# Expert remainders in pieces of 64 and twice 32 rows, four column groups, and the weights of two layers loaded apart

## The chip, the cores and the metric

The kernel runs on one core of one Trainium2 chip. A core has TensorE (PE in the profile, with its weight loads shown apart as PEld), VectorE (DVE), ScalarE (ACT), GpSimd (POOL) and SyncE (SP), which here issues most of the transfers. All data are 32-bit floats. The metric is the device time of one execution in microseconds (us). Most executions agree within 0.3%.

## The reference

The computation has two blocks, one behind the other. The first is causal attention over 8 batches, 8 heads, 576 positions and 64 elements a head, with a bias that grows with the running sum of a gate:

```python
scores = scale * np.matmul(q, k.transpose(0, 1, 3, 2))
cum = np.cumsum(np.maximum(s, 0.0), axis=-1)
bias = -(cum[:, :, :, None] - cum[:, :, None, :])
scores = np.where(causal, -1000000000.0, scores + np.minimum(bias, 0.0))
attn = softmax(scores)           # exp(scores - max) / (sum + 1e-9)
attn_out = np.matmul(attn, v)    # becomes x: 8 x 576 tokens of 512
```

The second is a layer of 8 experts. Each of the 4608 tokens goes to exactly one expert, either the one with the highest logit or, where a local gate says so, the one that the token before it went to:

```python
e = fresh_e if s == 0 or local_gate[b, s] < 0.5 else prev_e
h = np.maximum(x[b, s] @ w1[e], 0.0)     # w1[e]: 512 x 1024
out[b, s] = p[e] * (h @ w2[e])           # w2[e]: 1024 x 512
```

How many tokens an expert gets depends on the data. The inputs come from a fixed seed, so it is the same in each run.

## The kernel before

**Attention** (`attention`, L670 to L1035) takes 32 pairs of heads. Scores are computed transposed (L873), exponentiated on ScalarE (L874), masked on GpSimd (L859) and multiplied with the weighted values (L900). The exponentials are taken without subtracting a maximum, so this fast form holds only within a range of the gate sums. While it runs, the router (`Router`, L109 to L404) finds the expert of each token and scatters the token's row into a table in memory that has one region per expert (L308).

**Counting and assigning.** All shapes in the program are fixed, but the number of rows of an expert is not. So the program holds a fixed list of units, `ORDER` (L52), and the router works out on the chip, from the counts, which expert and which rows each unit gets. There are three kinds of unit. D takes 256 rows of one expert, S 128 rows of one expert, and M takes two pieces of 64 rows, which may belong to two experts. 14 D, 4 S and 6 M make 38 slots of 128 rows; 4608 rows are 36. `assign` (L339) hands out the places of one size: from `n`, the pieces that each expert wants, and `k`, the places there are, it computes the expert and first row of each place, how many pieces each expert got, and the running sum `end` of what was wanted. D's are handed out first, partly ahead of time (`EARLY`), then S's, then halves. The pieces wanted come from the counts by a shift (`shifted`, L327), for halves after adding 63, so that the last piece is rounded up:

```python
n = self.shifted("n3", 6, HALF - 1)                       # L400
v.scalar_tensor_tensor(n, self.used, -2.0, n, Alu.mult, Alu.add)
self.parts, _, end = self.assign("d", n, self.start, UNITS_OF["H"], HALF)
v.tensor_scalar(self.over, end[:, E - 1 :], -float(UNITS_OF["H"]), 0.0, Alu.add, Alu.max)   # L404
```

**The units' work** (`Experts`, L407 to L667). For a unit, SP fetches its rows from the table (`fetch`, L470, L481), VectorE turns them in blocks of 32 (`turn_x`, L501), and SP loads the weights of the expert: `load` (L454, L467), 2 MB for layer 1 and 2 MB for layer 2. For D and S, layer 1 keeps the weights in TensorE and moves the rows (L525). For M, the rows are kept instead, 64 columns wide in one of two column groups, and the weights of the two experts move through them (L516). Its result is turned back by VectorE (`turn_h`, L536). Layer 2 (L551) keeps the rows and moves the weights, for M again in two column groups. VectorE multiplies with the gate (L554) and GpSimd scatters the rows to the output (L556); rows that fill up a unit without belonging to a token are not written.

**The order** is written out by hand (`run`, L564). An M is interleaved with the unit ahead of it: layer 1 of both, then layer 2 of both. There are four places for weights; a load goes to a place (`place`, L451) when the unit that used it is through. `loads` issues the next loads, both layers of one at once, as soon as that unit is in `done`; the fourth place opens only when the last rows have been scattered to the table. SP runs its queue in order.

**The guard.** `in_range` (L1048) checks that the fast attention was in range, adds `over`, the halves that were wanted beyond the 12 there are, and writes `out_of` (L1067). At the end every engine loads it and branches (L92 to L94):

```python
with tc.If(wrong > 0):
    attention_general(tc, q, k, vm, vt, s, w_gate, w_local, cum_d, x_d, ident, lg)   # L104
    route(tc, ident, lg, ebi, idx_g, idx_s, gate)
    experts_general(tc, w1, w2, out, x_d, ident, ebi, idx_g, idx_s, gate)            # L106
```

The general kernel computes the whole output for any input: attention with a row maximum (L1071 to L1303; for each pair of heads, scores in five steps, sums and maxima on VectorE, exponentials on ScalarE, transposes through TensorE, then the values; the inputs q, k and v of a batch have one buffer), routing (L1307), and 43 blocks of 128 rows (L1472 to L1548), each of two layers of eight 512-column products and twelve transposes.

Of the kernel before, what the change touches and what calls it, by code (L numbers as in the profile page):

```python
# [17 lines left out]
P = 128  # L18
B, H, S, DH = 8, 8, 576, 64
D = H * DH  # L20
# [27 lines left out]
EMPTY = 1 << 20  # L48
DOUBLE, SINGLE, HALF = 2 * P, P, P // 2
EARLY = (2, 3)  # L50
UNITS_OF = {"D": 14, "S": 4, "H": 12}
ORDER = "DDDDD" + "MDD" * 3 + "MDS" * 2 + "MDSS"  # L52
PLACES = 4
# [55 lines left out]
class Router:  # L109
# [273 lines left out]
    def assign_doubles(self):  # L383
        v = self.nc.vector
        self.counted()
        n = self.shifted("n1", 8)
        v.tensor_tensor(n, n, self.used, op=Alu.subtract)
        v.tensor_scalar(self.start, self.used, float(DOUBLE), None, Alu.mult)
        self.doubles, used, _ = self.assign("b", n, self.start, UNITS_OF["D"] - sum(EARLY), DOUBLE)
        v.tensor_tensor(self.used, self.used, used, op=Alu.add)  # L390
        v.tensor_scalar(self.start, self.used, float(DOUBLE), None, Alu.mult)

    def assign_rest(self):
        v = self.nc.vector
        n = self.shifted("n2", 7)
        v.scalar_tensor_tensor(n, self.used, -2.0, n, Alu.mult, Alu.add)
        self.singles, used, _ = self.assign("c", n, self.start, UNITS_OF["S"], SINGLE)
        v.scalar_tensor_tensor(self.used, self.used, 2.0, used, Alu.mult, Alu.add)
        v.tensor_scalar(self.start, self.used, float(SINGLE), None, Alu.mult)
        n = self.shifted("n3", 6, HALF - 1)  # L400
        v.scalar_tensor_tensor(n, self.used, -2.0, n, Alu.mult, Alu.add)
        self.parts, _, end = self.assign("d", n, self.start, UNITS_OF["H"], HALF)
        self.over = self.t("over", [P, 1])
        v.tensor_scalar(self.over, end[:, E - 1 :], -float(UNITS_OF["H"]), 0.0, Alu.add, Alu.max)  # L404


class Experts:  # L407
    def __init__(self, ctx, tc, w1, w2, out, table, router):
        self.ctx, self.tc, self.nc = ctx, tc, tc.nc
        self.w1, self.w2, self.out, self.table, self.router = w1, w2, out, table, router  # L410

        def pool(name, bufs):
            return ctx.enter_context(tc.tile_pool(name=name, bufs=bufs))

        self.w_first = pool("w_first", 1)
        self.xqs = pool("xqs", 2)
        self.xts = pool("xts", 2)
        self.sm = pool("sm", 4)
        self.x_stack = ExitStack()
        self.p_x = self.x_stack.enter_context(tc.tile_pool(name="p_x", bufs=2 * GB, side="right"))  # L420
        self.puts = []
        self.units = []
        count = {"D": 0, "S": 0, "M": 0}
        loads = 0
        for kind in ORDER:
            n = 2 if kind == "M" else 1
            self.units.append((kind, count[kind], list(range(loads, loads + n))))
            count[kind] += 1
            loads += n
        assert count == {"D": UNITS_OF["D"], "S": UNITS_OF["S"], "M": UNITS_OF["H"] // 2}  # L430
        self.owner = {l: u for u, (_, _, ls) in enumerate(self.units) for l in ls}
        self.ws, self.xq, self.gi, self.xT, self.hT, self.hs = {}, {}, {}, {}, {}, {}

    def piece(self, u, i, row):
        kind, n, _ = self.units[u]
        if kind == "D":
            if n < sum(EARLY):
                i = int(n >= EARLY[0])
                of, n = self.router.early[i], n - i * EARLY[0]
            else:  # L440
                of, n = self.router.doubles, n - sum(EARLY)
        elif kind == "S":
            of = self.router.singles
        else:
            of, n = self.router.parts, 2 * n + i
        return self.nc.values_load(of[0:1, row, n : n + 1], engines=[ET.SP], min_val=0,
                                   max_val=E * CAP if row else E - 1,
                                   skip_runtime_bounds_check_because="clamped when it was counted")
# [4 lines left out]

    def load(self, l, part=None):  # L454

        if l not in self.owner:
            return
        nc, u = self.nc, self.owner[l]
        if not part:
            pool = getattr(self, self.place(l))  # L460
            self.ws[l] = pool.tile([P, DK, F], F32, name="w1b"), pool.tile([P, FK, D], F32, name="w2b")
            self.e = self.piece(u, self.units[u][2].index(l), 0)
        parts = 1 if part is None else 4
        for t, src in zip(self.ws[l], (self.w1, self.w2)):
            n = t.shape[1] // parts
            c = slice((part or 0) * n, (part or 0) * n + n)
            nc.sync.dma_start(t[:, c].rearrange("p c f -> p (c f)"),  # L467
                              src[bass.ds(self.e, 1), :, c].rearrange("o p c f -> (o p) (c f)"))

    def fetch(self, u):  # L470
# [6 lines left out]
        gi = self.gi[u] = self.sm.tile([P, 2, 2], F32, name="gi")  # L477
        pieces = 2 if kind == "M" else 1

        def get(to, of):  # L480
            self.tc.add_to_no_dep_group("gets", nc.sync.dma_start(to, of).ins)  # L481

        size = {"D": DOUBLE, "S": SINGLE, "M": HALF}[kind]
        for i in range(pieces):
            r = self.piece(u, i, 1)
            src = self.table[bass.ds(r, size)]
            t = size // 32
            for a in range(4):
                get(xq[32 * a : 32 * a + 32, i * t : i * t + t, :],
                                  src[:, a, :].rearrange("(t i) f -> i t f", i=32))  # L490
            p = min(size, P)
            get(gi[i * HALF : i * HALF + p, :n, :],
                              src[:, 0, XW - 2 :].rearrange("(n p) f -> p n f", p=p))

    def turn_x(self, u):
        if u >= len(self.units):
# [5 lines left out]
                                 xq[:, :n, : P].rearrange("p t (c i) -> p t c i", i=32))  # L502

    def layer1(self, u, c):
        nc, mm = self.nc, self.nc.tensor.matmul
        kind, _, ls = self.units[u]
        xT = self.xT[u]
        if kind == "M":
            if c == 0:
                self.hs[u] = self.fp.tile([P, F], F32, name="hs")  # L510
            if c < 2:
                ps = self.ps_m.tile([P, 512], F32, name="hp", tag="m")
                for k in range(DK):
                    for i in range(2):
                        d = slice(HALF * i, HALF * i + HALF)
                        mm(ps[d, :], lhsT=xT[:, k, d], rhs=self.ws[ls[i]][0][:, k, c * 512 : c * 512 + 512],  # L516
                           start=(k == 0), stop=(k == DK - 1))
                nc.scalar.activation(self.hs[u][:, c * 512 : c * 512 + 512], ps, Act.Relu)  # L518
# [10 lines left out]
    def turn_h(self, u):  # L529
        if self.units[u][0] != "M":  # L530
            return
# [8 lines left out]
    def layer2(self, u, between=None):  # L540
# [4 lines left out]
        for n in range(2 if kind == "D" else 1):  # L545
            ps = self.ps_y.tile([P, D], F32, name="yp")
            for k in range(FK):
                for i in range(2 if kind == "M" else 1):
                    w = HALF if kind == "M" else P
                    d = slice(i * w, i * w + w)  # L550
                    mm(ps[d, :], lhsT=hT[:, k, n * P + i * w : n * P + i * w + w], rhs=self.ws[ls[i]][1][:, k, :],  # L551
                       start=(k == 0), stop=(k == FK - 1))
# [11 lines left out]
    def run(self, recs, wend, out_of):  # L564
# [44 lines left out]
        self.load(2)  # L609
        loaded, done, fetched, freed = 3, set(), 2, False  # L610

        def loads():
            nonlocal loaded, freed
            while loaded in self.owner:
                if before.get(loaded) is not None and self.owner[before[loaded]] not in done:
                    return
                if self.place(loaded) == "w_last" and not freed:
                    if self.puts or todo:
                        return
                    self.x_stack.close()  # L620
                    self.w_last = pool("w_last", 1, side="right")
                    freed = True
                self.load(loaded)
                loaded += 1

# [14 lines left out]
        while u < len(kinds):  # L640
            if u + 1 < len(kinds) and kinds[u + 1] == "M":
                order += [(1, u), (1, u + 1), (2, u), (2, u + 1)]
# [4 lines left out]
        for what, u in order:  # L647
            if what == 1:
# [9 lines left out]
                if u:  # L658
                    self.turn_x(u + 1)
                    if u + 3 < first or not (self.puts or todo):  # L660
                        fetches(u + 3)
                        loads()
            else:
                self.layer2(u, lambda: between(u))
                done.add(u)
                loads()
        assert not todo and not self.puts  # L667


def attention(ctx, tc, q, k, vm, vt, vT, s, wbd_in, ident, recs, wend, router, experts):  # L670
# [290 lines left out]
    for i in range(4):  # L961
        plan(n + 9 + i, 3, lambda i=i: experts.load(0, i))
    plan(n + 12, 1, lambda: (experts.fetch(0), experts.fetch(1)))
# [643 lines left out]
```

## Time and profile before

| what | us |
|---|---|
| median of 3 runs | 774.21 (773.25 to 776.68) |
| the profiled execution | 774.9 |
| its span, first to last instruction | 773.1 |
| TensorE busy in the span | 760.7 |
| attention, up to the first expert product | 234.5 |
| expert products, 234 to 766: TensorE busy | 532.0 |
| end after the last product | 7 |

In the profile, a line such as `L551 PE MATMUL` names the line of the kernel. A 32-bit product is shown as two records, so `x16` in the chain of work is eight products. The chain is the work that ended last, followed back from the end; a slice line shows the busy share of 40 equal slices in tenths; a DMA line shows a queue's packets, its MB, and its share of the 16 DMA engines' time.

### The profile page before, as it was taken

Reading aid. Unit: us, or ns where it says so; the run is one execution under the profiler, and the core shown is the slowest. Engines: PE = TensorE matmul, PEld = TensorE weight load, DVE = VectorE, ACT = ScalarE, POOL = GpSimd, SP = SyncE. Lnnn points to the kernel's source line nnn. Section 1 sums busy time; section 2 is a strip of 40 time slices with the busy share of each in tenths; the row PEclk is TensorE's granted clock in tenths of the full one; section 3 lists DMA queues with packets and bytes.
Section 4 is the critical chain, followed back from the end, with each engine's and each line's share of the span. In section 5 each row is a group of like instructions: output and inputs, shape, how many; then the busy total and the mean of one; then the engine's idle time right before and its main releaser. Section 6 shows DMA issues by size and latency. Waiting matters only on the chain.

```text
span 773.1 us, 15685 instructions
## 1 busy us (share of the span) xinstructions
PE 760.7 (98%) x6319; PEld 512.9 (66%) x6319; DVE 247.4 (32%) x690; ACT 163.2 (21%) x315; POOL 216.1 (28%) x457
## 2 busy tenths in 40 slices
PE   8999999999999999999999999999999999999996
PEld 5887888888787657656376456737554664664664
DVE  5645655656644532110401320040113005005010
ACT  4454345344341001001010100101010110110111
POOL 3662276586666245430101010000101011001000
PEclk9999999999999999999999999999999999999999
DMA  8756557758678877639389739937982995996900
GB/s 299 270 204 219 184 165 257 231 172 301 203 245 325 277 272 268 235 87 413 96 341 391 235 115 430 382 99 272 420 276 54 412 382 174 418 383 220 404 16 32
DMA packets 57298, 196.74 MB, mean 254 GB/s; under 512 B 11901, under 2 KB 33149, under 8 KB 48000
## 3 DMA queue, kind: packets, MB, share of 16 engines
q1 hardware_dynamic: 50336, 175.55, 63.2%
q0 software_dynamic: 6880, 20.10, 6.7%
q8 instruction: 52, 0.85, 0.5%
q14 instruction: 30, 0.25, 0.1%
HBM read 175.00 MB, written 21.14 MB: 254 GB/s over the span
## 4 chain that ended last, share of the span: by engine, by line
PE 95%; DVE 2%; POOL 1%; issue 1%; ACT 1%; POOLq 0%
PE yp L551 34%; PE hp L525 29%; PE po L900 13%; PE ps L873 11%; PE hp L516 5%; PE vwp L814 1%; POOL e L859 1%; PE warm L747 0%; ACT e L874 0%; POOL table L308 0%; DVE vg L832 0%; DVE xb L908 0%; PE pos L260 0%; DVE mi L226 0%; PE lp L192 0%
## 5 line engine op out<-in xcount | busy, mean ns | idle before, releaser
L551 PE MATMUL yp<-w2b,hT 128*128 128x512 f32 (+1 forms) x704 | 267.4, 594 | 0.0
L525 PE MATMUL hp<-xT,w1b 128*128 128x256 f32 (+1 forms) x1152 | 226.0, 357 | 0.0
L525 PEld LDWEIGHTS hp<-xT,w1b 128*128 128x128 f32 x1152 | 198.8, 190 | 32.5 <-issue 9.9
L551 PEld LDWEIGHTS yp<-w2b,hT 128*128 128x128 f32 (+1 forms) x704 | 110.2, 175 | 148.8 <-issue 146.8
L556 POOL DMA_INDIRECT out_dram<-y,gi x38 | 37.1, 975 | 431.8 <-DVE y L554 367.5
L527 ACT ACTIVATE hT<-hp 128x256 f32<-128x256 f32 (+1 forms) x144 | 51.8, 359 | 435.7 <-PE hp L525 306.3
L554 DVE TENSOR_SCALAR y<-yp,gi 128x512 f32<-128x512 f32 x38 | 28.3, 744 | 296.1 <-PE yp L551 296.1
L874 ACT ACTIVATE e<-ps 128x768 f32<-128x768 f32 (+1 forms) x128 | 97.5, 837 | 109.5 <-PE ps L873 102.5
L900 PE MATMUL po<-vg,e 128*64 128x75 f32 x3200 | 116.0, 229 | 1.6 <-issue 1.4
L900 PEld LDWEIGHTS po<-vg,e 128*64 128x64 f32 x3200 | 108.8, 136 | 6.4 <-issue 2.8
L873 PE MATMUL ps<-qb,kb 64*128 64x192 f32 (+4 forms) x768 | 98.6, 400 | 1.6 <-DVE recs L906 1.2
L873 PEld LDWEIGHTS ps<-qb,kb 64*128 64x128 f32 x768 | 67.7, 187 | 32.9 <-ACT e L874 9.7
L308 POOL DMA_INDIRECT table<-xb,idx x72 | 74.0, 1028 | 28.8 <-issue 26.3
L859 POOL TENSOR_SCALAR_AFFINE_SELECT e<-e 128x256 f32<-128x256 f32 (+1 forms) x160 | 63.7, 425 | 51.6 <-ACT e L874 50.5
L536 DVE STREAM_TRANSPOSE hT<-hs 32x256 f32<-32x256 f32 x96 | 41.8, 436 | 108.6 <-ACT hs L518 107.3
L516 PE MATMUL hp<-w1b,xT 128*64 128x512 f32 x192 | 42.5, 595 | 0.0
L906 DVE RECIPROCAL recs<-po 128x12 f32<-128x12 f32 x64 | 13.2, 207 | 80.7 <-PE po L900 75.6
L908 DVE TENSOR_TENSOR xb<-po,recs 128x384 f32<-128x384 f32 x64 | 29.3, 458 | 3.9 <-POOL gap L307 1.1
L516 PEld LDWEIGHTS hp<-w1b,xT 128*64 128x64 f32 x192 | 13.3, 137 | 25.5 <-issue 25.3
L832 DVE TENSOR_TENSOR vg<-va,wk 128x1024 f32<-128x1024 f32 (+1 forms) x21 | 29.7, 1416 | 0.7 <-DMA va<-in_vm_dram 0.7
L501 DVE STREAM_TRANSPOSE xT<-xq 128x1024 f32<-128x1024 f32 (+1 forms) x24 | 24.4, 1016 | 0.6 <-issue 0.4
L307 POOL COPY gap<-recs 1x1 f32<-1x1 f32 x39 | 11.1, 284 | 30.9 <-DVE recs L906 30.9
(218 smaller groups left out, 185.9 us busy)
## 6 DMA issues: line engine op xcount, KB each, us to landing
w1b<-in_w_dram SPq DMA_DIRECT2D x29, 2048.0 KB
w2b<-in_w_dram SPq DMA_DIRECT2D x29, 2048.0 KB
kb<-in_k_dram SPq DMA_DIRECT2D x32, 288.0 KB
qb<-in_q_dram SPq DMA_DIRECT2D x32, 288.0 KB
vTb<-in_vT_dram SPq DMA_DIRECT2D x7, 1280.0 KB
xq<-table SPq DMA_DIRECT2D x56, 130.0 KB
va<-in_vm_dram SPq DMA_DIRECT2D x7, 1024.0 KB
w1b<-in_w_dram SPq DMA_DIRECT2D x4, 512.0 KB
```

Source lines behind the costliest of these rows:

```text
L308: put = self.nc.gpsimd.indirect_dma_start(out=self.halves, in_=src, element_offset=0, in_offset=None, out_offset=bass.IndirectOffsetOnAxis ...
L516: mm(ps[d, :], lhsT=xT[:, k, d], rhs=self.ws[ls[i]][0][:, k, c * 512 : c * 512 + 512], start=(k == 0), stop=(k == DK - 1))
L525: mm(ps[:, :w], lhsT=self.ws[ls[0]][0][:, k, c * P : c * P + P], rhs=xT[:, k, :w], start=(k == 0), stop=(k == DK - 1))
L527: nc.scalar.activation(self.hT[u][:, c, :w], ps[:, :w], Act.Relu)
L536: self.nc.vector.transpose(hT[32 * a : 32 * a + 32, :, 32 * r : 32 * r + 32], hs[32 * r : 32 * r + 32].rearrange("p (c i) -> p c i", i=P)[ ...
L551: mm(ps[d, :], lhsT=hT[:, k, n * P + i * w : n * P + i * w + w], rhs=self.ws[ls[i]][1][:, k, :], start=(k == 0), stop=(k == FK - 1))
L556: put = nc.gpsimd.indirect_dma_start(out=self.out[:, :], out_offset=bass.IndirectOffsetOnAxis(ap=gi.bitcast(I32)[:, n, 0:1], axis=0), in_= ...
L832: nc.vector.tensor_tensor(vgs[b % 2][g][:, c0:c1].rearrange("p c h e -> p (c h) e")[:, :, :DH], va[:, c0:c1].rearrange("p c h e -> p (c h) ...
L859: nc.gpsimd.affine_select(out=ap, in_=ap, compare_op=Alu.is_ge, fill=0.0, base=base, pattern=n, channel_multiplier=-1)
L873: mm(ps[:, h, at : at + z - a], lhsT=kb[d, key : key + P], rhs=qb[d, a:z], start=True, stop=True)
L874: nc.scalar.activation(e, ps, Act.Exp, scale=scale)
L900: mm(po[d, j - j0, :], lhsT=weights_of(n, c, j, h), rhs=vg[:, c, 2 * hp + h, :], start=(c == 0), stop=(c == last))
```

## The change

The remainder of an expert, what is left after its pieces of 256 and 128 rows, goes into pieces of 64 and of 32 rows. A new unit, T, holds one piece of 64 and two of 32 rows. In a T the rows stand in four column groups of 32, where the first two belong to the piece of 64 (`groups`). The list of units becomes a string of 25, written out. It holds 16 D, 5 S, 1 M and 3 T, which is 41 slots of 128 rows by count; the summary that came with the change speaks of 37 slots in place of 38. `UNITS_OF` is now counted from the string. `assign_rest` hands out halves after rounding the count down, then quarters after rounding up, and `over` is what is wanted of quarters beyond the places. `load` can load one layer's weights alone, and `loads` keeps two positions, one per layer: the first layer's weights of a load may be asked for once layer 1 of the unit that held the place is through.

```diff
-DOUBLE, SINGLE, HALF = 2 * P, P, P // 2
+DOUBLE, SINGLE, HALF, QUARTER = 2 * P, P, P // 2, P // 4
-UNITS_OF = {"D": 14, "S": 4, "H": 12}
-ORDER = "DDDDD" + "MDD" * 3 + "MDS" * 2 + "MDSS"
+PIECES = {"D": (DOUBLE,), "S": (SINGLE,), "M": (HALF, HALF), "T": (HALF, QUARTER, QUARTER)}
+ORDER = "DDDDDTDDDTDDDTDDMDSDSDSSS"
+UNITS_OF = {size: sum(PIECES[u].count(size) for u in ORDER) for size in (DOUBLE, SINGLE, HALF, QUARTER)}
...
-        self.singles, used, _ = self.assign("c", n, self.start, UNITS_OF["S"], SINGLE)
+        self.singles, used, _ = self.assign("c", n, self.start, UNITS_OF[SINGLE], SINGLE)
         v.scalar_tensor_tensor(self.used, self.used, 2.0, used, Alu.mult, Alu.add)
         v.tensor_scalar(self.start, self.used, float(SINGLE), None, Alu.mult)
-        n = self.shifted("n3", 6, HALF - 1)
+        n = self.shifted("n3", 6)
         v.scalar_tensor_tensor(n, self.used, -2.0, n, Alu.mult, Alu.add)
-        self.parts, _, end = self.assign("d", n, self.start, UNITS_OF["H"], HALF)
+        self.parts, used, _ = self.assign("d", n, self.start, UNITS_OF[HALF], HALF)
+        v.scalar_tensor_tensor(self.used, self.used, 2.0, used, Alu.mult, Alu.add)
+        v.tensor_scalar(self.start, self.used, float(HALF), None, Alu.mult)
+        n = self.shifted("n4", 5, QUARTER - 1)
+        v.scalar_tensor_tensor(n, self.used, -2.0, n, Alu.mult, Alu.add)
+        self.quarters, _, end = self.assign("q", n, self.start, UNITS_OF[QUARTER], QUARTER)
         self.over = self.t("over", [P, 1])
-        v.tensor_scalar(self.over, end[:, E - 1 :], -float(UNITS_OF["H"]), 0.0, Alu.add, Alu.max)
+        v.tensor_scalar(self.over, end[:, E - 1 :], -float(UNITS_OF[QUARTER]), 0.0, Alu.add, Alu.max)
...
-    def load(self, l, part=None):
+    def load(self, l, layer=None, part=None):
...
+        for i, src in enumerate((self.w1, self.w2)):
+            if layer is not None and layer != i:
+                continue
...
+    def groups(self, u):
+
+        kind, _, ls = self.units[u]
+        w = {"M": HALF, "T": QUARTER}.get(kind, P)
+        at = [l for l, size in zip(ls, PIECES[kind]) for _ in range(min(size, P) // w)]
+        return [(slice(i * w, i * w + w), l) for i, l in enumerate(at)]
...
                 for k in range(DK):
-                    for i in range(2):
-                        d = slice(HALF * i, HALF * i + HALF)
-                        mm(ps[d, :], lhsT=xT[:, k, d], rhs=self.ws[ls[i]][0][:, k, c * 512 : c * 512 + 512],
+                    for d, l in self.groups(u):
+                        mm(ps[d, :], lhsT=xT[:, k, d], rhs=self.ws[l][0][:, k, c * 512 : c * 512 + 512],
                            start=(k == 0), stop=(k == DK - 1))
...
         def loads():
-            nonlocal loaded, freed
-            while loaded in self.owner:
-                if before.get(loaded) is not None and self.owner[before[loaded]] not in done:
-                    return
...
+            more = True
+            while more:
+                more = False
+                for layer in range(2):
+                    l = loaded[layer]
+                    if l in self.owner and (not layer or l < loaded[0]) and ready(l, layer):
+                        self.load(l, layer)
+                        loaded[layer] += 1
+                        more = True
...
-            if u + 1 < len(kinds) and kinds[u + 1] == "M":
+            if u + 1 < len(kinds) and kinds[u + 1] in "MT":
...
             else:
                 self.layer2(u, lambda: between(u))
-                done.add(u)
-                loads()
+            done[what - 1].add(u)
+            loads()
```

More of the change, by code (lines that the diff above doesn't have):

```diff
@@ L388, in assign_doubles @@
         v.tensor_scalar(self.start, self.used, float(DOUBLE), None, Alu.mult)
-        self.doubles, used, _ = self.assign("b", n, self.start, UNITS_OF["D"] - sum(EARLY), DOUBLE)
+        self.doubles, used, _ = self.assign("b", n, self.start, UNITS_OF[DOUBLE] - sum(EARLY), DOUBLE)
         v.tensor_tensor(self.used, self.used, used, op=Alu.add)
@@ L422, in __init__ @@
         self.units = []
-        count = {"D": 0, "S": 0, "M": 0}
+        count = dict.fromkeys(UNITS_OF, 0)
         loads = 0
         for kind in ORDER:
[L426 to L430, printed above, removed]
+            at = []
+            for size in PIECES[kind]:
+                at.append((size, count[size]))
+                count[size] += 1
+            self.units.append((kind, at, list(range(loads, loads + len(at)))))
+            loads += len(at)
         self.owner = {l: u for u, (_, _, ls) in enumerate(self.units) for l in ls}
@@ L434, in piece @@
     def piece(self, u, i, row):
-        kind, n, _ = self.units[u]
-        if kind == "D":
+        size, n = self.units[u][1][i]
+        r = self.router
+        if size == DOUBLE:
             if n < sum(EARLY):
-                i = int(n >= EARLY[0])
-                of, n = self.router.early[i], n - i * EARLY[0]
-            else:
-                of, n = self.router.doubles, n - sum(EARLY)
-        elif kind == "S":
-            of = self.router.singles
+                j = int(n >= EARLY[0])
+                of, n = r.early[j], n - j * EARLY[0]
+            else:
+                of, n = r.doubles, n - sum(EARLY)
         else:
-            of, n = self.router.parts, 2 * n + i
+            of = getattr(r, {SINGLE: "singles", HALF: "parts", QUARTER: "quarters"}[size])
         return self.nc.values_load(of[0:1, row, n : n + 1], engines=[ET.SP], min_val=0,
@@ L452, in place @@
         return ("w_first", "w_rest", "w_rest")[l] if l < 3 else ("w_first", "w_rest", "w_rest", "w_last")[(l - 3) % PLACES]
-    def load(self, l, part=None):
+    def load(self, l, layer=None, part=None):
         if l not in self.owner:
             return
-        nc, u = self.nc, self.owner[l]
+        u = self.owner[l]
         if not part:
-            pool = getattr(self, self.place(l))
-            self.ws[l] = pool.tile([P, DK, F], F32, name="w1b"), pool.tile([P, FK, D], F32, name="w2b")
             self.e = self.piece(u, self.units[u][2].index(l), 0)
         parts = 1 if part is None else 4
-        for t, src in zip(self.ws[l], (self.w1, self.w2)):
-            n = t.shape[1] // parts
+        for i, src in enumerate((self.w1, self.w2)):
+            if layer is not None and layer != i:
+                continue
+            ws = self.ws.setdefault(l, [None, None])
+            if not part:
+                pool = getattr(self, self.place(l))
+                ws[i] = pool.tile([P, FK, D] if i else [P, DK, F], F32, name=f"w{i + 1}b")
+            n = ws[i].shape[1] // parts
             c = slice((part or 0) * n, (part or 0) * n + n)
-            nc.sync.dma_start(t[:, c].rearrange("p c f -> p (c f)"),
-                              src[bass.ds(self.e, 1), :, c].rearrange("o p c f -> (o p) (c f)"))
+            self.nc.sync.dma_start(ws[i][:, c].rearrange("p c f -> p (c f)"),
+                                   src[bass.ds(self.e, 1), :, c].rearrange("o p c f -> (o p) (c f)"))
     def fetch(self, u):
@@ L477, in fetch @@
         gi = self.gi[u] = self.sm.tile([P, 2, 2], F32, name="gi")
-        pieces = 2 if kind == "M" else 1
         def get(to, of):
             self.tc.add_to_no_dep_group("gets", nc.sync.dma_start(to, of).ins)
-        size = {"D": DOUBLE, "S": SINGLE, "M": HALF}[kind]
-        for i in range(pieces):
+        first = 0
+        for i, size in enumerate(PIECES[kind]):
             r = self.piece(u, i, 1)
             src = self.table[bass.ds(r, size)]
-            t = size // 32
+            t = slice(first // 32, (first + size) // 32)
             for a in range(4):
-                get(xq[32 * a : 32 * a + 32, i * t : i * t + t, :],
-                                  src[:, a, :].rearrange("(t i) f -> i t f", i=32))
+                get(xq[32 * a : 32 * a + 32, t, :], src[:, a, :].rearrange("(t i) f -> i t f", i=32))
             p = min(size, P)
-            get(gi[i * HALF : i * HALF + p, :n, :],
-                              src[:, 0, XW - 2 :].rearrange("(n p) f -> p n f", p=p))
+            get(gi[first : first + p, :n, :], src[:, 0, XW - 2 :].rearrange("(n p) f -> p n f", p=p))
+            first += size
     def turn_x(self, u):
@@ L507, in layer1 @@
         xT = self.xT[u]
-        if kind == "M":
+        if kind in "MT":
             if c == 0:
@@ L529, in turn_h @@
     def turn_h(self, u):
-        if self.units[u][0] != "M":
+        if self.units[u][0] not in "MT":
             return
@@ L547, in layer2 @@
             for k in range(FK):
[L548 to L551, printed above, removed]
+                for d, l in self.groups(u):
+                    mm(ps[d, :], lhsT=hT[:, k, n * P + d.start : n * P + d.stop], rhs=self.ws[l][1][:, k, :],
                        start=(k == 0), stop=(k == FK - 1))
@@ L609, in run, with ready @@
         self.load(2)
-        loaded, done, fetched, freed = 3, set(), 2, False
-        def loads():
-            nonlocal loaded, freed
-            while loaded in self.owner:
-                if before.get(loaded) is not None and self.owner[before[loaded]] not in done:
-                    return
[L617 to L624, printed above, removed]
+        loaded, done, fetched, freed = [3, 3], (set(), set()), 2, False
+        def ready(l, layer):
+            nonlocal freed
+            if before.get(l) is not None and self.owner[before[l]] not in done[layer]:
+                return False
+            if self.place(l) == "w_last" and not freed:
+                if self.puts or todo:
+                    return False
+                self.x_stack.close()
+                self.w_last = pool("w_last", 1, side="right")
+                freed = True
+            return True
+        def loads():
+            more = True
[7 more added lines that the diff above has]
+                        more = True
         def fetches(u):
@@ L661, in run @@
                         fetches(u + 3)
-                        loads()
             else:
                 self.layer2(u, lambda: between(u))
-                done.add(u)
-                loads()
+            done[what - 1].add(u)
+            loads()
         assert not todo and not self.puts
@@ L961, in attention @@
     for i in range(4):
-        plan(n + 9 + i, 3, lambda i=i: experts.load(0, i))
+        plan(n + 9 + i, 3, lambda i=i: experts.load(0, None, i))
     plan(n + 12, 1, lambda: (experts.fetch(0), experts.fetch(1)))
```

## The prediction

> **What bounds the kernel now.** First the page: span, busy time, slices.
>
> ```profile
> span 773.1 us, 15685 instructions
> PE 760.7 (98%) x6319; PEld 512.9 (66%) x6319; DVE 247.4 (32%) x690; ACT 163.2 (21%) x315; POOL 216.1 (28%) x457
> PE   8999999999999999999999999999999999999996
> PEclk9999999999999999999999999999999999999999
> DMA  8756557758678877639389739937982995996900
> ```
>
> TensorE works through, at full clock, with short gaps at both ends. In 234 to 766 us (the experts) the table of windows has PE busy for 532.00 of 532.00 us, so no weight load is waited for, and the path there is the sum of the units' matmuls. Second view, the chain in order of time, gives one unit of each kind:
>
> ```profile
> 360.02 7.02 PE hp L516 x32
> 367.04 20.95 PE yp L551 x64
> 387.98 14.01 PE hp L525 x64
> 402.00 13.73 PE yp L551 x32
> 415.73 0.43 PE hp L525 x2
> ...
> 738.13 7.14 PE hp L525 x64
> 745.28 6.87 PE yp L551 x16
> ```
>
> A D (256 rows) costs 13.81 + 13.73 = 27.54 us, an S (128 rows) 7.14 + 6.87 = 14.01, an M (two 64s in two column groups) 7.02 + (20.95 - 13.73) = 14.24, and the layer 1 after an M 0.20 more (14.01 against 13.81).
>
> Third, what a reader might skip: whether the rows fit the units. Routing the reference's inputs gives 573, 516, 565, 575, 717, 459, 513, 690 rows for experts 0 to 7. If so, before's 14 D, 4 S and 12 halves leave the six M, in order, with 61+4, 53+63, 64+13, 64+11, 1+64 and 64+50 rows. Each row writes 2 KB of output. The transfers of the six M's scatters (packets, MB, share), each in a window around its own issue (389, 459, 528, 598, 655 and 713 us):
>
> ```profile
> q0 software_dynamic: 80, 0.13, 2.9%
> q0 software_dynamic: 80, 0.24, 4.6%
> q0 software_dynamic: 80, 0.16, 3.1%
> q0 software_dynamic: 80, 0.15, 2.5%
> q0 software_dynamic: 80, 0.13, 2.3%
> q0 software_dynamic: 80, 0.23, 5.8%
> ```
>
> 65, 116, 77, 75, 65 and 114 rows are 0.133, 0.238, 0.158, 0.154, 0.133 and 0.233 MB: all six agree, so I trust the counts. They use the 12 halves to the last one.
>
> Fourth, the guard. `over` (L404) goes into `out_of` (L1067); every engine loads it and branches at L94 past the general kernel:
>
> ```profile
> 275.56 0.15 DVE L404 TENSOR_SCALAR over<-dend 128x1 f32<-128x1 f32 x1
> ...
> L94 PEldq COMPARE_BRANCH  x1: 3676/3676/3676, 760.2 to 760.2; - x1
> L94 DVEq COMPARE_BRANCH  x1: 72/72/72, 766.8 to 766.8; - x1
> ```
>
> After that branch nothing is computed: the general kernel costs nothing today.
>
> **The change, part by part.**
>
> *The units.* The new string holds 16 D, 5 S, 1 M and 3 T: 41 slots of 128 rows, not the 37 of the summary. Against before: +2 D, +1 S, -5 M, +3 T = 55.08 + 14.01 - 71.20 + 3T. A T is 8 steps per layer part of four 128x512 matmuls in four column groups. Nearest row: the value-logit product, 128*32, puts 16 matmuls of 160 columns (32 records) into 1.23 us; one full-width column costs 6.87 us / (8 x 512) = 1.68 ns, so four ideal groups would take 16 x 160 x 1.68 / 4 = 1.07. A T lies between an M's 14.24 and 14.24 x 1.23/1.07 = 16.4; I take 14.5, nearer to the M since the matmuls have 512 columns, as the M's do. 3T = 43.5, fewer follow-ups (four M and T, not six) -0.4. Sum +41.0 us (40.2 to 46.7), all on the path.
>
> [...]
>
> *The weights, asked for apart.* 32 loads of 4 MB, not 30, and a new order in SP's queue; SP's weight issues (L467) waited 19.5 us for PE's layer 2 and 13.7 for layer 1, with the fetches queued behind them (POOL's scatter waited 45.9 us for fetched rows, PE never). A first-layer half can go when PE has read the old one. In the steady part, DDDT, six loads move 25.2 MB in 3 x 27.5 + 14.5 = 97 us, 260 GB/s; the stretches with DMA share near 1.0 moved 372 to 437 GB/s. So nothing is gained, as PE waits for nothing, and little lost. The tight place is the first T: its third weights need the place of unit 3 (done at 346), the fourth place opened at about 347, and 8.4 MB at 425 GB/s take 20 us while layer 1 would start at 360. Asked for first, the two first layers, with a second layer between, are in at about 362. I put 1 us there (0 to 8).
>
> *Fetches and router.* Three T with three pieces of five issues each are 45 issues against five M less with 10 each, 50; plus 3 units of 5: 10 more issues of some 0.4 us on SP, beside matmuls. A second `assign` is some 21 DVE instructions of 0.15 to 0.26 us, 4 us at 275 us, where DVE is idle 79% of the time: zero; without that cover 4 us.
>
> *Does it fit?* New `assign_rest`: the D's now hold all 15 whole 256s (16 places). Singles wanted 1 + 1 + 1 = 3 of 5. Remainders: 61, 4, 53, 63, 77, 75, 1, 50. Halves are now counted with `>> 6` and nothing added: only 77 and 75 ask for one, 2 of 5. Quarters are rounded up: 2, 1, 2, 2, 1 (13), 1 (11), 1, 2 = 12, and there are 6. Three halves stay empty while six quarters overflow: `over` = 12 - 6 = 6. So `out_of` is 6, the branch is not taken, and **the whole computation runs a second time in the general kernel** (L94 to L106).
>
> *What the general kernel costs.* No instruction of it is in the trace; I price its code by rows.
> Attention, 32 head pairs, per pair. VectorE: score sums (widths 128 to 512 and 576, two each) by 128x192 at 358 ns and 128x384 at 558, so 158 + 1.04 per element, 5.45 us; five maxima by reduces of 144 and 288 (297, 452 ns) 4.1; scaling 1.8: 11.3 us. ScalarE: exponentials by 768 at 809 and 896 at 920 ns, 4.1; copies by 256 at 383 and 512 at 597, 4.0; with the logits 8.9. GpSimd 2.3. TensorE: scores by the fast path's 2.95 us for 1600 columns a head, 3.4 for 1856; 25 transposes, 20 value products and 11 small ones of the logits, each between 104 ns (the five 64-column transposes in 0.52 us) and 223 (7.14 us / 32): 5.8 to 12.5; tail 0.7; so 10 to 16.6. A pair takes at least VectorE's 11.3, and 36 if nothing overlaps. The code interleaves pair n's scores with pair n-1's transposes, so I stay near the floor: 16. 32 x 16 = 512; the single buffer for q and k adds at seven batch changes a 2.36 MB load (6 to 9 us) plus the scaling (3), 9 net, 63; start 20. Attention 595 (410 to 880).
> Routing between: some 60 dependent small instructions at 0.2 to 0.4 us and ten of 0.5 to 1.25: 35 (25 to 60).
> Experts: 43 blocks, each 16 products of 512 columns at 0.859 (13.74) and 12 transposes (1.2 to 2.7); 15.7, 675 (645 to 760), start and end 15. 4.2 MB in 15.7 us is 267 GB/s, which before carries too.
> Sum 595 + 35 + 690 = **1320 us** (1095 to 1715).
>
> [...] Were attention's TensorE work at half rate throughout, its 13 us a pair would be 26 and the sum 10 x 32 = 320 us more.
>
> *The sum.* The profiled execution took 774.9 us (span 773.1 and 1.8 around it), 0.1% over the median of 774.21. 774.9 + 41 + 1 + 1320 = 2137; I say 2140.
>
> **The rivals.**
> *It fits after all.* Then only the units count: 774.9 + 42 = 817 us. For it: the summary speaks as if the rows fit. Against: 12 quarters wanted of 6, counts confirmed by six transfers.
> *Not slower: 37 slots.* Two D fewer than the string holds and remainders of 33 to 64 counted as halves (then 5 halves and 6 quarters, both exactly used) would give 1 S + 3 T - 5 M = 14.0 + 43.5 - 71.2 - 0.4 = -14 us, 761. It decides from the point where `over` is 0 and the string has 14 D; the diff says otherwise in both places.
> *General kernel slow:* attention at 24 us a pair or a half clock, with PE waiting at every step. +256 to +320 us: 2400 to 2460. For it: one buffer per input, engines waiting in order. Against: no gap of several us inside a pair.
>
> **How the numbers follow.** General kernel as priced 0.80, slow 0.12, fits 0.06, 37 slots 0.02. The first alone: 1950 to 2330. The range for 8 in 10 runs from 1920 (every lower bound is 774.9 + 40 + 1095 = 1910) to 2470 (the slow rival; all upper bounds together, 2545, are left out with the two small cases). A change under 0.5% cannot be told from none here (before's three runs lie 0.4% apart). Faster only with 37 slots, 0.02; same 0.01; slower 0.97.
>
> **What would show it.** Right: line groups of the general kernel (scores, `ptp`, `htp`, `x_tokens`) fill the span from about 810 us; 41 us more of expert matmuls ahead of that; 64 records in each T's first layer in 7.0 to 8.2 us; no PE idle over 8 us near 360; in the second half attention near 595 us, experts near 16 us a block. Wrong: a span that ends near 815 or 760 (the guard was not reached, so a count or my reading of the rounding is off); or attention there far from 16 us a pair, which is the least certain term.

## The result and the profile after

| | us |
|---|---|
| before, beside it on the same chip | 774.99 (773.25 to 776.68) |
| changed kernel | 2171.55 (2165.25 to 2182.35) |
| ratio | 2.8035, 95% interval 2.7904 to 2.8167 |
| forecast | 2140 (1920 to 2470) |

The profiled execution of the changed kernel took 2165.25 us, its span 2163.3. The page, first lines:

```profile
span 2163.3 us, 32563 instructions
PE 2006.1 (93%) x12683; PEld 1293.3 (60%) x12683; DVE 706.8 (33%) x1595; ACT 556.7 (26%) x1338; POOL 399.8 (18%) x765
PE   9999998898989997988898889885999999999997
PEclk9999999999999998878898989885999999999999
```

Twice the instructions: the program ran two kernels. The guard's branch in the changed kernel shows it: each engine passes it, and then comes to a second branch 1300 us later, at the end of the block. Each of the general kernel's two layers has 688 records of products, 43 blocks of 16:

```profile
L95 PEldq COMPARE_BRANCH  x2: 87/134/180, 840.2 to 2145.5; - x2
L95 DVEq COMPARE_BRANCH  x2: 51/53/55, 846.8 to 2152.1; - x2
```

```profile
L1547 PE MATMUL hp<-w1b,xT 128*128 128x512 f32 x688 | 311.0, 595 | 0.8 <-DVE xT L1537 0.8
L1563 PE MATMUL yp<-w2b,hT 128*128 128x512 f32 x688 | 302.4, 592 | 0.3 <-ACT hT L1557 0.3
```

Where the time went, by the first and last records of each part:

| part | forecast | measured |
|---|---|---|
| first kernel, last product, against 766.2 before | +42 | +79.9 (846.1) |
| general kernel, attention | 595 | 603 (to 1449) |
| routing, until the first block's product | 35 (the blocks' start is in the next row) | 54 (to 1503) |
| 43 blocks | 690 with start and end | 649 (to 2152) |
| general kernel, all | 1320 | 1306 |

The general kernel was priced 14 us too high and the first kernel 38 too low. Those 38 us are what the experiments are mostly about. TensorE's timeline in the changed kernel (start, length, work, idle before it and what ended that) shows them:

```profile
358.79 1.06 PE L530 MATMUL hp<-w1b,xT 128*32 128x512 f32 x6
366.59 8.64 PE L530 MATMUL hp<-w1b,xT 128*32 128x512 f32 x58 [6.74 <-DMA w1b<-in_w_dram]
375.17 21.00 PE L563 MATMUL yp<-w2b,hT 128*128 128x512 f32 x96
396.10 14.08 PE L539 MATMUL hp<-xT,w1b 128*128 128x256 f32 x64
418.29 17.02 PE L563 MATMUL yp<-w2b,hT 128*128 128x512 f32 x32 [8.11 <-DMA w2b<-in_w_dram]
...
525.97 16.10 PE L563 MATMUL yp<-w2b,hT 128*128 128x512 f32 x32 [7.34 <-DMA w2b<-in_w_dram]
...
635.42 15.98 PE L563 MATMUL yp<-w2b,hT 128*128 128x512 f32 x32 [10.05 <-DMA w2b<-in_w_dram]
```

The first T waits 6.74 us in its first layer. Behind each of the three T's, the next D waits 7.3 to 10.1 us for its second layer's weights. Before, no unit waited at all (532.00 of 532.00 us busy). After each such wait the products run slow for a while: the 32 records of a D's second layer take 17.02, 16.10 and 15.98 us where they take 13.90 elsewhere, and the granted clock is 0.50 in the first 5 us behind the wait of 8.11 (418.3 to 423.3). The waits sum to 32.2 us; the slow stretches behind them add some 10 (2.6 + 3.1 + 2.2 + 2.1).

### The profile page after: what moved, and what is told of

Its sections match the earlier page's. It is cut to its first block, busy times and chain, and to the rows that moved or that the text cites. A ratio compares the mean times of both kernels' runs of the same rounds, so it can differ in the third digit from the quotient of the medians.

```text
span 2163.3 us, 32563 instructions
## 1 busy us (share of the span) xinstructions
PE 2006.1 (93%) x12683; PEld 1293.3 (60%) x12683; DVE 706.8 (33%) x1595; ACT 556.7 (26%) x1338; POOL 399.8 (18%) x765
## 5 line engine op out<-in xcount | busy, mean ns | idle before, releaser
L563 PE MATMUL yp<-w2b,hT 128*128 128x512 f32 (+2 forms) x816 | 293.5, 603 | 25.5 <-DMA w2b<-in_w_dram 25.5
L1547 PE MATMUL hp<-w1b,xT 128*128 128x512 f32 x688 | 311.0, 595 | 0.8 <-DVE xT L1537 0.8
L1563 PE MATMUL yp<-w2b,hT 128*128 128x512 f32 x688 | 302.4, 592 | 0.3 <-ACT hT L1557 0.3
L1563 PEld LDWEIGHTS yp<-w2b,hT 128*128 128x128 f32 x688 | 130.6, 190 | 164.6 <-issue 164.1
L1547 PEld LDWEIGHTS hp<-w1b,xT 128*128 128x128 f32 x688 | 127.9, 191 | 145.7 <-issue 144.5
L1210 ACT ACTIVATE sc<-sc,st 128x128 f32<-128x128 f32 (+3 forms) x256 | 142.3, 557 | 107.9 <-DVE st L1207 107.9
L1254 PE MATMUL po<-vb,pt 128*128 128x64 f32 x1280 | 166.9, 280 | 1.7 <-ACT pt L1239 1.7
L1254 PEld LDWEIGHTS po<-vb,pt 128*128 128x128 f32 x1280 | 164.0, 203 | 2.5 <-ACT pt L1239 2.4
L1183 PE MATMUL ps<-kb,qb 64*128 64x384 f32 (+3 forms) x512 | 129.4, 592 | 28.8 <-DMA kb<-in_k_dram 26.8
L1186 DVE SCALAR_TENSOR_TENSOR sc<-cb,cq,ps 128x128 f32<-128x128 f32 (+3 forms) x256 | 126.6, 541 | 89.8 <-PE ps L1183 87.0
```

The lines of the kernel that those rows point to most:

```text
L563: mm(ps[d, :], lhsT=hT[:, k, n * P + d.start : n * P + d.stop], rhs=self.ws[l][1][:, k, :], start=(k == 0), stop=(k == FK - 1))
L1183: mm(ps[:, h, :w], lhsT=qb[d, hp, t * P : w], rhs=kb[d, hp, :w], start=True, stop=True)
L1186: nc.vector.scalar_tensor_tensor(sc[:, h], cb[:, h, :w], cq[:, c : c + 1], ps[:, h, :w], Alu.subtract, Alu.add)
L1210: nc.scalar.activation(sc[:, h], sc[:, h], Act.Exp, bias=st[:, 0, c : c + 1], accum_out=st[:, 1, c : c + 1])
L1254: mm(po[:, h, :], lhsT=pt[h * (t + 1) + c], rhs=vb[:, c, 2 * hp + h, :], start=(c == 0), stop=(c == t))
L1547: mm(ps, lhsT=xT[i][:, c, :], rhs=ws[i][0][:, c, f], start=(c == 0), stop=(c == DK - 1))
```

## The experiments

Each is compared with the kernel before on the same chip, which took 770.6 to 771.6 us there, some 0.5% less than above.

**Is it the overflow?** Halves rounded with 31 added, nothing else.

```diff
-        n = self.shifted("n3", 6)
+        n = self.shifted("n3", 6, QUARTER - 1)
```

> The halves' count is rounded with QUARTER - 1 added, nothing else; then 5 halves and 6 quarters are exactly used and the guard stays at 0. Theory (the general kernel runs because six quarters overflow): the first part ends at 846 us as in the changed kernel and the exit takes its usual 9 us, 855 us in all. Rival (the extra time lies elsewhere, the overflow is not its cause): near 2170 us.

Measured: 851.85 us, ratio 1.1036 (1.1010 to 1.1062). One argument took 1320 us off. Six experts now ask for a half, five get one, the sixth (50 rows) takes two quarters, and six quarters are wanted of six. The overflow is the cause of the second run, and without it the change still makes the kernel 10% slower.

**What does the general kernel cost by itself?** The kernel before, with its guard told that six halves are missing:

```diff
-        v.tensor_scalar(self.over, end[:, E - 1 :], -float(UNITS_OF["H"]), 0.0, Alu.add, Alu.max)
+        v.tensor_scalar(self.over, end[:, E - 1 :], -float(UNITS_OF["H"] - 6), 0.0, Alu.add, Alu.max)
```

> The kernel before with its limit of halves lowered by 6 in the guard alone, so that it reports an overflow of 6 though all rows have been placed. Theory (the general kernel costs the same 1306 us wherever it is entered, and the first part of the changed kernel the other 80): 766 + 1306 + 11 = 2083 us. Rival (the new units make the second part dearer or cheaper): off by more than 20 us.

Measured: 2083.38 us. From the end of the first kernel's products at 761.7 to those of the second at 2064.5 are 1303 us, against 1306 in the changed kernel. So the second run's price is the same with and without the new units, within 3 us.

**Is it the order of the weight requests?** The rounded kernel with both layers asked for together, `loads` and its calls as in the kernel before:

```diff
-        loaded, done, fetched, freed = [3, 3], (set(), set()), 2, False
+        loaded, done, fetched, freed = 3, set(), 2, False
...
-            done[what - 1].add(u)
-            loads()
+                done.add(u)
+                loads()
```

> As the rounded kernel, but both layers' weights are asked for together, as before the change. Theory (what made the first part late is the order of the requests: behind a T three first layers go ahead of the second layer that is needed next): the waits of 8, 7 and 10 us and the slow clock behind them go, only the first T's wait of 7 us stays, 815 to 825 us. Rival (a T needs three loads in places that are still taken, whatever the order): 850 us or more.

Measured: 848.11 us, ratio 1.0989 (1.0964 to 1.1014). My theory, that asking apart made the waits, fell. Behind the same three T's, TensorE now waits for the next D's first layer instead of its second one:

```profile
399.04 16.51 PE L539 MATMUL hp<-xT,w1b 128*128 128x256 f32 x64 [6.07 <-DMA w1b<-in_w_dram]
...
504.77 16.55 PE L539 MATMUL hp<-xT,w1b 128*128 128x256 f32 x64 [6.19 <-DMA w1b<-in_w_dram]
...
614.06 16.52 PE L539 MATMUL hp<-xT,w1b 128*128 128x256 f32 x64 [9.71 <-DMA w1b<-in_w_dram]
```

**Is asking apart harmful by itself?** The units of before, halves rounded up and no quarters, with the change's `loads`:

```diff
-ORDER = "DDDDDTDDDTDDDTDDMDSDSDSSS"
+ORDER = "DDDDD" + "MDD" * 3 + "MDS" * 2 + "MDSS"
-        n = self.shifted("n3", 6)
+        n = self.shifted("n3", 6, HALF - 1)
...
-        v.tensor_scalar(self.over, end[:, E - 1 :], -float(UNITS_OF[QUARTER]), 0.0, Alu.add, Alu.max)
+        v.tensor_scalar(self.over, end[:, E - 1 :], -float(UNITS_OF[HALF]), 0.0, Alu.add, Alu.max)
```

> The units of before (14 D, 4 S, 6 M) with only the requests for the two layers' weights taken apart. Theory (the order of the requests costs where a unit frees several places at once): an M frees two, not three, so one first layer less is ahead; up to 4 us at each of six M, 775 to 797 us. Rival (the order is harmless and the T's cause the waits): 774 us, within 0.5%.

Measured: 770.51 us, ratio 0.9995 (0.9981 to 1.0009): no difference, as the rival had it. With these units, TensorE is busy without a gap either way (525.50 of 525.50 us from 234.5 to 760). So the wait came with the T's, and the question became what about them.

A T and the D that it is interleaved with hold four loads, which are all the places there are. The next D's weights can go only where that D's were. SP's timeline of the rounded kernel in this stretch shows when they are asked for:

```profile
365.79 0.35 SPq L477 DMA_DIRECT2D w1b<-in_w_dram  x1
381.81 1.89 SPq L490 DMA_DIRECT2D xq<-table  x4
390.53 0.40 SPq L490 DMA_DIRECT2D gi<-table  x1
391.50 2.17 SPq L477 DMA_DIRECT2D w1b<-in_w_dram  x3
394.23 3.37 SPq L477 DMA_DIRECT2D w2b<-in_w_dram  x4
```

At 366 the first layer for the next D goes out. Then SP comes to a fetch, whose `gi` needs a buffer that is free only when a scatter to the output has landed, at 390. Everything behind it stands. Then three first layers go, not needed before 421 (a layer 2 of 13.7 us later), and only then the second layer that is needed at 407.5 (the D's first layer starts at 393.46 and takes 14.01). That is four transfers of 2.1 MB at the 397 GB/s measured from 391.5 to 416, 21 us from 391.5: 413 by this count, and the product began at 416. Two runs took one of these apart each.

**Order alone:** nothing asked for after a T's or an M's layer 1, and second layers first.

```diff
-                for layer in range(2):
+                for layer in (1, 0):
...
-            loads()
+            if what == 2 or kinds[u] not in "MT":
+                loads()
```

> The rounded kernel with one change to the requests: nothing is asked for after a T's layer 1, and after a layer 2 second layers go first. So the second layer of the D behind the T is asked for ahead of three first layers. Theory (queue order): it lands by 400 us, before it is needed at 408; 26 us of waits and 7 us of slow clock behind them go, 819 us. Rival (bandwidth: the transfers behind a T are too many whatever their order): 840 us or more.

Measured: 820.09 us, ratio 1.0620 (1.0583 to 1.0656). The three waits are gone, only the first T's is left. The same fetch stands ahead on SP, yet one second layer goes first now:

```profile
391.94 0.40 SPq L490 DMA_DIRECT2D gi<-table  x1
392.92 0.35 SPq L477 DMA_DIRECT2D w2b<-in_w_dram  x1
393.78 2.08 SPq L477 DMA_DIRECT2D w1b<-in_w_dram  x3
396.41 2.51 SPq L477 DMA_DIRECT2D w2b<-in_w_dram  x3
```

**The fetch alone:** six buffers for `gi`.

```diff
-        self.sm = pool("sm", 4)
+        self.sm = pool("sm", 6)
```

> The rounded kernel with six buffers for gi, not four, so that a fetch on SP no longer waits until a scatter to the output has landed. Theory (the weight requests behind a T stand behind that fetch, and the order costs only with that delay): the three first layers go out at 381 instead of 391 and the second layer behind them lands near 403, before 408: about 820 us. Rival (the fetch is not what holds them): 850 us.

Measured: 832.93 us, ratio 1.0780 (1.0752 to 1.0808). The requests go out at 386.6, not at 381 as I had expected (the fetch still waits for the turned rows of the unit ahead, until 383), and the three waits shrink to 2.6, 3.2 and 4.1 us, from 8.4, 7.3 and 10.3 in the rounded kernel. So the fetch is some 4 to 6 us of each wait, and the order is enough by itself to remove them. Of these shorter waits the first cost no more than itself and the second did: behind the first the 32 records take 13.97 us, near the 13.90 without a wait, behind the second 15.67.

```profile
411.25 13.97 PE L563 MATMUL yp<-w2b,hT 128*128 128x512 f32 x32 [2.59 <-DMA w2b<-in_w_dram]
...
511.70 15.67 PE L563 MATMUL yp<-w2b,hT 128*128 128x512 f32 x32 [3.17 <-DMA w2b<-in_w_dram]
```

**Do 37 slots help as they stand?** The rounded kernel with two D fewer:

```diff
-ORDER = "DDDDDTDDDTDDDTDDMDSDSDSSS"
+ORDER = "DDDDDTDDTDDTDDMDSDSDSSS"
```

> The rounded kernel with the string DDDDDTDDTDDTDDMDSDSDSSS: 14 D, 37 slots. Two D less are 55 us. Theory (waits behind a T come from its places and its queue, not from the number of D): 852 - 55 = 797 us, still over the kernel before by 3%. Rival (waits grow where a T comes every two D, as more weights are due in less time): 805 us or more. A third, that with 37 slots the units' sum shows, would be 757 us.

Measured: 808.40 us, ratio 1.0476 (1.0443 to 1.0509). The rival was right: with two D between T's, the waits grow to 13.7, 12.9 and 10.4 us. They ate 12 of the 55 us and keep it 4.8% slower than the kernel before.

**A version without waits.** 37 slots with three D between T's, the first T one D later, halves rounded, requests held, six buffers:

```diff
-ORDER = "DDDDDTDDDTDDDTDDMDSDSDSSS"
+ORDER = "DDDDDDTDDDTDDDTDMDSSSSS"
```

> 14 D, 5 S, 1 M, 3 T as DDDDDDTDDDTDDDTDMDSSSSS (37 slots, the first T one D later), halves rounded, requests held as above, six buffers for gi. Theory (with no wait for weights the sum of the units shows): the kernel before less 14 us, 757 us of 771. Rival (a T with a D takes all four places, so a wait stays behind each): 770 us or more.

Measured: 754.59 us, ratio 0.9769 (0.9743 to 0.9796). TensorE is busy for 511.00 of the 511.00 us from 234 to 745, at a granted clock of 1.00, and one T stands in the chain as

```profile
383.69 7.00 PE hp L530 x64
390.69 20.93 PE yp L563 x96
411.63 14.01 PE hp L539 x64
```

so a T costs 7.00 + (20.93 - 13.73) = 14.20 us. The gain of 17 us is near the units' sum of 14; an S ahead of an M, which made two M's of before some 0.9 us longer each (at 638.46 in the kernel before, 15.01 for an S's and an M's second layer together, and 15.01 - 6.87 = 8.14 for the M's, not the 20.95 - 13.73 = 7.22 behind a D), is gone from the order too.

Two more runs asked which part of that version it is: both layers together again, and requests and buffers as in the change.

> The 754.6 us kernel (order DDDDDDTDDDTDDDTDMDSSSSS, six buffers for gi) with both layers' weights asked for together again. Theory (a T and its D fill all four places, so the next D's first layer must be asked for after layer 1 of that D, ahead of the T): the waits of 6 to 10 us for first layers, seen when the rounded kernel asked together, come back behind three T's, less about 5 us each for the fetch that no longer stands ahead: 757 to 770 us. Rival (the order of units alone gave the gain): 754 us.

> The same order of units, with requests and gi buffers as in the change. Theory (queue order behind a T): the first T's wait is gone but 8 to 10 us and 2 to 3 of slow clock come back behind each T: 785 us, over the kernel before. Rival (the order of units alone gave the gain): 755 us.

Measured: 764.52 us, ratio 0.9913 (0.9894 to 0.9933), and 774.47 us, ratio 1.0043 (1.0029 to 1.0057). In the first, the waits did not come back behind the T's as I had expected (0.3 us in all there), but the M, late in the order, waits 6.3 us for a first layer; the time is inside my range for another reason than mine. In the second, waits for second layers are back, 7.2 and 7.9 us behind the first two T's and 0.7 later, 15.8 us together; the time is 10 us below the 785 that I had expected, and the first T's own wait is gone. So the order of units alone gains nothing over the kernel before, though it is worth some 33 us against the other string of the same 37 slots (808.40). Asking apart, in the order of need, is worth some 10 us here. Where the layers are asked for apart, held requests and six buffers together are worth some 20; no run of this string asks apart with only one of the two, so their shares are open here.

## Why the prediction was right, and where it was off

**The direction and the size** came from the step "Does it fit?": counts from the reference, checked against the bytes of six scatters, put through the new rounding. The rounded kernel and the forced guard both confirm it: one removes the second run, the other makes it without the change.

**The general kernel**, priced only from rows of other instructions, came to 1320 and took 1306. Attention: 595 forecast, 603 measured, from parts that were off both ways. A pair at a granted clock of 1.00 took about 14 us (969.54 to 983.28), less than my 16; but pairs at a lower clock took 17.5 to 21 (952.01 to 969.54 at 0.76, 870.56 to 891.82 at 0.68), so the mean with the batch changes was 18.4 (588 us from the first score at 861, over 32), against 18.0 forecast ((512 + 63) / 32). The rival of a slow general kernel was half right. The clock did fall, to 0.88 over attention, but TensorE did not wait at every step: it was busy for 89% of it. The half clock throughout, which gave the 320 us in that rival and with it the range's upper end, was my assumption, and no run shows it: 0.50 was granted in stretches, 0.88 over attention. The single buffer per input is one reason, as I gave it: at a batch change TensorE waits 3.86 us for `kb`, and the granted clock is 0.50 for the next 7 us (924.7 to 932). But the clock falls at one batch's logits too (0.66 from 943 to 963), where TensorE hardly waits (19.59 of 20 us busy; shown at the end). Blocks: 649 / 43 = 15.1 us against 15.7; transposes, 15.1 - 13.74 = 1.4 us a block, cost less than the middle of my bounds. (The bound of 760 for the blocks is not what its terms give: 43 x (13.74 + 2.7) = 707.) Routing was 54, not 35: it ran at a granted clock of 0.50 and its table products alone took 17.75 us. That the total came within 1.5% of the median is luck in part: one term was 14 us too high, another 38 too low.

**The step that failed** is "The weights, asked for apart". I put 1 us (0 to 8) there and measured 42, with 32 of waiting and 10 of slow clock. Asking apart is not the cause by itself, since the rounded kernel waits as well with both layers asked for together (848 us). What makes the waits is a T that takes three of the four places, while the requests go out in the wrong order and behind a fetch that is held up. I looked at the first T alone; its wait, 6.7 us, is inside my bounds. For the later T's I compared mean demand with mean rate, 260 against 372 to 437 GB/s, and that was the mistake: the mean says nothing where all four places are held by one pair of units and open at once. I had the pieces in hand, the fetches queued on SP and the order of the requests, and didn't follow one D's second layer through them. The 42 us was hidden in the total by the 14 us that the general kernel came out cheaper and by a range set by that larger term. In the rival "It fits after all" it shows plainly: I gave 42 us over the kernel before, and the rounded kernel took 81, or 48 with the requests in order. Of those 48, 10 are the first T's wait and the slow clock behind it, which leaves 38 for the units. I had 41.0 for them; the T's are 0.9 less, and the two M's behind an S in the kernel before, which I priced like the others, are 1.8.

**The T** was taken at 14.5 between 14.24 and 16.4 and measured 14.20: four column groups lose nothing here against two (7.00 us for the first layer, 7.02 in an M of before). The 32 products, of 0.859 us each one by one, take 7.00 in four groups (3.93x).

**The rival of 37 slots** was worked out as 761 us. The units' sum is right (754.6 reached), but the change's string with two D struck out, also 37 slots, took 808, since the waits are not in that sum. Its condition, an overflow of 0 and 14 D, was not enough.

## What to carry to other kernels

Where a kernel holds a fixed plan for data-dependent sizes and a guard behind it, put the actual counts through the plan before anything else: rounding the larger piece down and the smaller up overflowed with three of five larger places empty, and only the time, 2.8 times as long, and the doubled count of instructions showed it. A buffer count is checked at the unit that takes most of the buffers, by following the next unit's transfer from the moment its place opens, through what stands ahead of it on its queue, to the product that needs it; a mean rate can't show such a wait. Requests on one queue go out in the order in which they are needed.

## What the hardware showed that I had not expected

TensorE was busy and slow here. In the general kernel's attention, the stretch with the logits has it busy for 19.59 of 20 us at a granted clock of 0.66. The table of windows of the changed kernel, with PE and its weight loads, the other engines, and then the clock, says so in its first line; the second is the routing, the third the blocks of 512-column products:

```profile
943.00:963.00 20.00, 19.59 (x116) 15.98 (x113) 5.81 (x16) 7.02 (x21) 1.22 (x3) 0.66 0.54 178
...
1448.90:1503.10 54.20, 24.36 (x105) 20.64 (x104) 24.99 (x63) 1.10 (x2) 12.44 (x14) 0.50 0.27 111
1503.10:2151.90 648.80, 648.52 (x1888) 315.86 (x1888) 86.39 (x127) 72.10 (x129) 81.04 (x81) 1.00 0.77 301
```

Up to 952 us TensorE does transposes and 9-column products there, and the clock falls among them: eight records of the same product go from 0.96 to 1.72 us with no wait between. The next pair's scores, transposes and value products, from 952 on, still run at 0.62 up to 963. The third line below is from the routing, TensorE's longest piece of work there:

```profile
945.13 0.96 PE L1285 MATMUL lps<-wg,pt 128*128 128x9 f32 x8
...
948.57 1.72 PE L1285 MATMUL lps<-wg,pt 128*128 128x9 f32 x8
...
1474.08 17.75 PE L1480 MATMUL table<-val,place 128*128 128x86 f32 x80 [12.64 <-POOL val L1478]
```

No run here separates the transposes in the logits' stretch from the very short products. But the clock was slow without transposes too: the routing's 80 records are products of 86 columns with no transpose among them, TensorE is busy in them for 17.75 us on end, and the granted clock stays at 0.50 from 1474 to 1492. The blocks' products of 512 columns, by contrast, start at 0.50 (1503.1 to 1506) and are at 0.94 in the next 4 us. What held the clock down in the logits and the routing, no run here shows.

And the late weights cost more than the waits: behind the waits of 8.11, 7.34 and 10.05 us the 32 records of a second layer took 3.1, 2.2 and 2.1 us more than 13.90, and the first T's products 2.6 more behind its 6.74, which together was a quarter of what the late weights cost here. The wait of 2.59 us with six buffers had no such price (13.97 us behind it); those of 3.17 and 4.06 had 1.8 us (15.67 each).
